# Foldings in pairs: two small weight products issued back to back instead of one at a time

## The chip, the cores and the metric

The kernel runs on one core of one Trainium2 chip. The metric is the time of one execution in device microseconds (us). The core's engines have queues of their own, each worked off in order: TensorE (PE in the profile, its weight loads PEld), VectorE (DVE), ScalarE (ACT), GpSimd (POOL) and SyncE (SP). Matrix products are written to PSUM, the memory behind TensorE, which is divided into banks; the other engines read them there.

## The reference, cut to what matters

Three stages follow each other on 8 batches of 576 tokens (8 heads of 64 in 512 columns):

```python
k_m = einsum('bhsm,bhsd->bhmd', a, k)          # a: softmax of phi over the tokens, 32 memories a head
v_m = einsum('bhsm,bhsd->bhmd', a, v)
attn = softmax(q @ k_m.T / 8)                  # 576 x 32 a head
x = attn @ v_m                                 # stage 1 input: 4608 x 512
x = (silu(x @ w_gate) * (x @ w_val)) @ w_out   # first feed-forward, 1536 hidden columns
out = elu(x @ w_in) @ w_out2                   # second feed-forward, 2048 hidden columns
```

The kernel never forms `attn @ v_m`. It multiplies `v_m` of a batch (the tile `vt`) into the gate and value weights (`WG`) first, and the result (`VW`) is then multiplied with `attn`. This small product is called a folding here.

## The kernel before, in words

A folding is `vw(b, p)`: for batch `b` and the pair `p` of hidden units (a unit is 128 hidden columns; units 0 to 3, pairs 0 and 1, belong to the first stage, pairs 2 to 5 to the second), eight matmuls of 64 rows by 32 columns write 128 x 1024 numbers into two PSUM banks (`pvw`). The profile counts each of the eight as two, so a folding is a row x16. Their shape uses a part of TensorE's array each, so that the eight work side by side; all matmuls of the feed-forwards use the whole array (128*128 in the rows). Then ScalarE copies the banks, rounded, into the upper half of `VW` (L265), and VectorE subtracts this copy from the banks for the lower half (L266). Only after the subtraction may TensorE write these banks again. There are 48 foldings, of which 46 are emptied in this way.

**First stage** (one pass for each batch `b`): gate and value products of units 0 to 3 (`pg`, `pv`, twice 6 matmuls of 288 columns for each unit and half), their output products (`pd`), and between them, one task after each unit's step (`todo`, `tick`), the attention of the next batches: transposes (`ps_aT`, `ps_kvT`), memories (`ps_kvm`), scores (`ps_sc`) and, at the end of the list, the two foldings for batch `b + 1` (`vw_tasks`). Both foldings use the bank pair `ps_kv` in turn. Scores use the bank pair `ps_at`.

**Second stage**: four runs `n` of two batches, 16 units each (`units`). The output product of run `n` is done in 14 steps (`down_steps`, a product of seven is two steps, `acc` in the rows, 24 matmuls a step: 12 for each of two token halves `hf`) and lies between the units of run `n + 1`. One unit is 12 `pg` matmuls, a Silu on ScalarE (L701), 12 `pv` matmuls and a product on VectorE (L703). In this mixture `pg`, `pv` and `pvw` take turns on two bank pairs (the list `turn`: 1, 0, 1, 0, ...), and `acc` holds the other two. After every second unit one folding is issued (`vw2`), for the pair of units that comes two pairs later. The rounded halves of what the output product reads are made ahead by ScalarE (`hh`, L767) and VectorE (`hl`, L768), and VectorE also forms the sums between operands (L771) and prepares the third stage's weights in the background (`uq`, `uw`, `wc`).

The framework's scheduler settles the order in each engine's queue before the kernel runs: it takes the instruction that is ready first in its own estimate of times, by rank among those that are ready. `tc.issue_after(x)` keeps what follows behind `x` in that order, and `tc.high_priority()` raises its rank. On the chip each queue is then worked off in exactly that order.

Of the kernel before, what the change touches and what calls it, by code (L numbers as in the profile page):

```python
# [8 lines left out]
F32 = mybir.dt.float32  # L9
F32R = mybir.dt.float32r  # L10
# [3 lines left out]
ALU = mybir.AluOpType  # L14
# [24 lines left out]
def attention_moe_moe(ctx: ExitStack, tc: tile.TileContext, qT, phiT, kv, kv4, w1g, w1o, w2, out):  # L39
# [208 lines left out]
    VW = {}  # L248
# [1 line left out]

    def vw(b, p, pool=None, ps=None):
        t = VW[b, p] = vx_p.tile([128, 2, 2, 512], F32R, tag="vx", name="vw")
        both = ps or pool.tile([128, 2, 512], F32, tag="at", name="pvw")
        ps = [both[:, g] for g in range(2)]

        def head(j, g):
            r, c = slice(64 * g, 64 * g + 64), slice(32 * j, 32 * j + 32)
            return mm(ps[g][c], lhsT=Bs[b].vt[r, j, :], rhs=WG[p][j][r], start=True, stop=True)  # L260

        together([lambda j=j, g=g: head(j, g) for j in reversed(range(KD)) for g in (1, 0)])
        if b >= NEG or p >= UA // 2:
            with tc.high_priority() if pool is None else nullcontext():
                act(out=t[:, 0], in_=both, func=AF.Copy)  # L265
                tt(out=t[:, 1], in0=both, in1=t[:, 0].bitcast(F32), op=ALU.subtract)  # L266
            return
        for g in range(2):
            last["vwh"] = act(out=t[:, 0, g, :], in_=ps[g], func=AF.Copy)
        for g in range(2):  # L270
            mm(ps[g], lhsT=minus, rhs=t[:, 0, g, :], start=False, stop=True, skip_group_check=True)
            last["vwl"] = act(out=t[:, 1, g, :], in_=ps[g], func=AF.Copy)
            if g == 0:
                last["vwl0"] = last["vwl"]
# [10 lines left out]
    def down(ps, w, hs, ms, start, stop, skip=False):  # L285
        mm(ps, lhsT=w[0][:, ms], rhs=hs[0], start=start, stop=False, skip_group_check=skip)  # L286
        mm(ps, lhsT=w[1][:, ms], rhs=hs[0], start=False, stop=False, skip_group_check=skip)  # L287
        mm(ps, lhsT=w[0][:, ms], rhs=hs[1], start=False, stop=stop, skip_group_check=skip)  # L288

    def split_h(pool, h, n):  # L290
        hh = pool.tile([128, n], F32R, tag="hh", name="hh")
# [228 lines left out]

    G2 = ps_kv

    def vw_tasks(b):
        for p in range(UA // 2):
            yield lambda p=p: vw(b, p, G2)
# [67 lines left out]
    for b in range(B):  # L593
# [32 lines left out]
        if b == 0:  # L626
            v = list(vw_tasks(1))
            todo += [bk[0], bk[1], v[0], lambda: Bs[2].phi(), bk[2], bk[3], bk[4], v[1], fr[0], fr[1], bk[5]] + fr[2:] + [lambda: Bs[3].phi()]
        else:
            for i in range(max(len(bk), len(fr))):  # L630
                todo += fr[i:i + 1] + bk[i:i + 1]
            if b + 1 < B:
                todo += vw_tasks(b + 1)
        done = [0, 0]
        spread = 18 if b == 0 else 16 if b < B - 2 else 24

# [61 lines left out]
    def unit2(b, u, out):  # L698
        pg = up2(b, u, 0, "pg")
        s = t_p.tile([128, 2, HS], F32, tag="s", name="s")  # L700
        last["gate"] = act(out=s, in_=pg, func=AF.Silu)  # L701
        pv = up2(b, u, 128, "pv")
        last["h"] = stt(out=out, in0=s, scalar=1.0, in1=pv, op0=ALU.mult, op1=ALU.mult)  # L703

    def vw2(b, p):
        if len(turn) > MIX:
            ps = bank2(3, "pvw")
        else:
            ps = bank2(turn.pop(0), "pvw")
        vw(b, p, ps=ps)  # L710


    held = {}
# [33 lines left out]
    def down_steps(n, g, steps, comb):  # L747
        acc = {}

        def step(j, name, r, k, chain, *dst):  # L750
            start = name in ("P1", "P2", "P5", "P4")[:4 if steps is ALONE else 3]
            if start and j == 0:
                acc[chain] = [bank2(i, "acc")[:, :, :HS] for i in ((0, 1) if chain == "D" else (2, 3))]
            behind = nullcontext() if steps is ALONE else tc.issue_after(unit_end[-LAG].ins)
            if steps is not ALONE:
                w = wo_p.tile([128, 2, 2, 256], F32R, tag="w", name="ws")
                nc.sync.dma_start(out=w.bitcast(F32), in_=d1_d[:, r, 2 * j:2 * j + 2])
            else:
                if j == 0:
                    acc["w"] = vx_p.tile([128, 4, 2, 256], F32R, tag="vx", name="ws")  # L760
                    last["ws"] = nc.sync.dma_start(out=acc["w"].bitcast(F32), in_=d1_d[:, r])
                w = acc["w"][:, 2 * j:2 * j + 2]
            for hf in range(2):
                hs = [hs_p.tile([128, 2, HS], F32R, tag=t, name=t) for t in ("hh", "hl")]
                x = g[k][:, hf, 2 * j:2 * j + 2]
                with tc.high_priority():
                    act(out=hs[0], in_=x, func=AF.Copy)  # L767
                    last["h"] = last["gate"] = tt(out=hs[1], in0=x, in1=hs[0].bitcast(F32), op=ALU.subtract)  # L768
                for o, a, b, f in comb.get((name, 2 * j + hf), []):
                    with tc.issue_after(last["h"].ins):  # L770
                        tt(out=g[o][:, f], in0=g[a][:, f], in1=g[b][:, f], op=ALU.add if (o, a, b) == (2, 2, 3) else ALU.subtract)  # L771
                for i, m in [(i, m) for i in range(2) for m in range(2)]:
                    with behind if hf + i + m == 0 else nullcontext():
                        down(acc[chain][m][:, hf], (w[:, i, 0], w[:, i, 1]), (hs[0][:, i], hs[1][:, i]),
                             slice(128 * m, 128 * m + 128), start and j + i == 0, j + i == 2, not start)
            if j == 1:
                add_part(acc[chain], [(2 * n + b, c) for b, c in dst],
                         name == "P4" if steps is ALONE else None)

        return [lambda a=a, j=j: step(j, *a) for a in steps for j in range(2)]  # L780
# [28 lines left out]
    load2(1)  # L809

    unit_end = []
    LAG = 1

    def units(n, g):
# [3 lines left out]
        def unit(i, k, u):  # L818
            b, p = pairs[8 * n + i]
            if u % UA == 0:  # L820
                g[k] = gh_p.tile([128, 2, UA, HS], F32, tag="gh", name="gh")
            unit2(b, u, g[k][:, :, u % UA])
            unit_end.append(last["pe"])
            done[0] += 1
            background(fs, n0 * (1 - done[0] / (12 if n == 0 else 16)))
            if u % 2 == 1:
                if 8 * n + i + 2 < len(pairs):
                    vw2(*pairs[8 * n + i + 2])
                if i in (5, 7) and n < B // 2 - 1:
                    load2(2 * n + 2 + i // 7, nc.gpsimd)  # L830

# [7 lines left out]
    for n in range(B // 2 - 1):  # L839
        us = units(n + 1, g[n + 1])  # L840
        for i, f in enumerate(down_steps(n, g[n], MIXED, MIXCOMB)):
            f()
            for _ in range(2 if i in (0, 12) else 1):
                us.pop(0)()
# [311 lines left out]
```

## Time and profile before

| what | value |
|---|---|
| median of 3 runs | 1426.08 us (1426.02 to 1429.0) |
| the profiled execution | 1427.93 us, span in the profile 1426.2 us |
| TensorE busy | 1401.3 us, 98% of the span |
| VectorE busy | 1136.1 us, 80% |
| ScalarE busy | 862.4 us, 60% |
| mean granted clock of TensorE | 0.995 of full speed |

The span runs from the first to the last instruction; the time of an execution has 1.7 us more around it. A busy share near 100% says that an engine has work issued nearly all the time. Where a stretch is meant, the view by stretches is the one to read: for each stretch it gives the time in it that each engine was busy.

### The profile page before, as it was taken

The page shows a single profiled execution, that of the slowest core. Times are in us where ns is not written, and L with a number is a line of the kernel's source. Part 1 is how long each engine was busy: PE and PEld are TensorE (multiplying, and loading weights), DVE is VectorE, ACT ScalarE, POOL GpSimd, SP SyncE. Part 2 cuts the span into 40 slices and gives each one's busy share as a digit, 9 for nine tenths or more (in the row PEclk, how much of TensorE's full clock was granted, in tenths as well). Part 3 has the DMA queues.
Part 4 walks back from the last instruction along what each step waited for, and adds up shares of the span by engine and source line. Part 5 has one row for each costly group of instructions (what it writes and reads, how often), then busy time and mean ns, then how long its engine had stood idle before and what let it go on. Part 6 is the DMA issues. An engine that isn't in the chain of part 4 may idle for free.

```text
span 1426.2 us, 23205 instructions
## 1 busy us (share of the span) xinstructions
PE 1401.3 (98%) x9259; PEld 1211.6 (85%) x9259; DVE 1136.1 (80%) x1452; ACT 862.4 (60%) x1254; POOL 44.8 (3%) x73
## 2 busy tenths in 40 slices
PE   6899999999999999999999999999999999999998
PEld 4787889988999999999988888888888888888887
DVE  7988978778798877877988578885889488957884
ACT  5665545544465555555666388557866587548843
POOL 0000000000000000000000000000000000000000
PEclk8999999999999999999999999999999999999999
DMA  9888512664789887888889756766686667566653
GB/s 378 326 298 292 208 72 101 230 233 175 237 251 309 284 240 232 274 241 287 267 291 364 269 188 206 280 214 189 201 282 219 190 202 265 215 210 203 213 201 132
DMA packets 89484, 337.65 MB, mean 237 GB/s; under 512 B 9376, under 2 KB 23712, under 8 KB 70048
## 3 DMA queue, kind: packets, MB, share of 16 engines
q1 hardware_dynamic: 55312, 254.04, 51.6%
q10 hardware_dynamic: 26880, 51.39, 9.8%
q0 software_dynamic: 7184, 30.74, 8.9%
q8 instruction: 73, 1.20, 0.3%
q14 instruction: 35, 0.29, 0.1%
HBM read 251.13 MB, written 85.00 MB: 236 GB/s over the span
## 4 chain that ended last, share of the span: by engine, by line
PE 93%; DVE 3%; ACT 2%; DMA 1%; issue 1%; ACTq 0%; SPq 0%; DVEq 0%
PE pu L877 12%; PE pu L879 12%; PE pu L878 12%; PE pd L877 5%; PE pd L879 5%; PE pd L878 5%; PE acc L288 4%; PE acc L286 4%; PE acc L287 4%; PE pv L281 3%; PE pg L281 3%; PE pv L283 3%; PE pv L282 3%; PE pg L283 3%; PE pg L282 3%; PE pvw L260 3%
## 5 line engine op out<-in xcount | busy, mean ns | idle before, releaser
L878 PE MATMUL pu<-xlo,w 128*128 128x512 f32 x672 | 261.4, 389 | 0.0
L877 PE MATMUL pu<-xhi,w 128*128 128x512 f32 x672 | 261.4, 389 | 0.0
L879 PE MATMUL pu<-xhi,w 128*128 128x512 f32 x672 | 261.4, 389 | 0.0
L906 ACT ACTIVATE xhi<-g 128x1024 fp32r<-128x1024 f32 x120 | 126.5, 1058 | 106.9 <-PE pu L879 64.3
L907 DVE TENSOR_TENSOR xlo<-g,xhi 128x1024 fp32r<-128x1024 f32 x120 | 145.0, 1220 | 40.7 <-ACT xhi L906 40.6
L879 PEld LDWEIGHTS pu<-xhi,w 128*128 128x128 f32 x672 | 126.1, 188 | 26.3
L878 PEld LDWEIGHTS pu<-xlo,w 128*128 128x128 f32 x672 | 126.1, 188 | 26.2
L877 PEld LDWEIGHTS pu<-xhi,w 128*128 128x128 f32 x672 | 126.1, 188 | 26.1
L287 PE MATMUL acc<-hh,ws 128*128 128x288 f32 x448 | 131.7, 296 | 0.0
L286 PE MATMUL acc<-hh,ws 128*128 128x288 f32 x448 | 131.5, 295 | 0.0
L288 PE MATMUL acc<-hl,ws 128*128 128x288 f32 x448 | 128.8, 297 | 0.0
L281 PE MATMUL pv<-at,vw 128*128 128x288 f32 x384 | 115.6, 301 | 2.4 <-DVE s L306 0.7
L281 PE MATMUL pg<-at,vw 128*128 128x288 f32 x384 | 116.7, 304 | 1.1 <-ACT p L579 0.5
L767 ACT ACTIVATE hh<-gh 128x576 fp32r<-128x576 f32 x112 | 76.0, 685 | 68.6 <-PE acc L287 50.8
L282 PE MATMUL pg<-at,vw 128*128 128x288 f32 x384 | 114.1, 297 | 0.9 <-DVE at L488 0.9
L283 PE MATMUL pg<-at,vw 128*128 128x288 f32 x384 | 113.6, 296 | 0.0
L282 PE MATMUL pv<-at,vw 128*128 128x288 f32 x384 | 113.6, 296 | 0.0
L283 PE MATMUL pv<-at,vw 128*128 128x288 f32 x384 | 113.5, 296 | 0.0
L877 PE MATMUL pd<-xhi,w 128*128 128x512 f32 x288 | 112.0, 389 | 0.0
L878 PE MATMUL pd<-xlo,w 128*128 128x512 f32 x288 | 112.0, 389 | 0.0
L879 PE MATMUL pd<-xhi,w 128*128 128x512 f32 x288 | 112.0, 389 | 0.0
L897 DVE SCALAR_TENSOR_TENSOR et<-et 128x1024 f32<-128x1024 f32 x72 | 87.8, 1219 | 28.8 <-ACT et L896 28.8
(161 smaller groups left out, 3226.9 us busy)
## 6 DMA issues: line engine op xcount, KB each, us to landing
w<-dnd SPq DMA_DIRECT2D x64, 1024.0 KB, 4.9
w<-upd SPq DMA_DIRECT2D x40, 1024.0 KB, 5.7
w<-upd SPq DMA_DIRECT2D x32, 768.0 KB, 4.6
ws<-d1d SPq DMA_DIRECT2D x42, 512.0 KB, 4.5
kvr<-kv SPq DMA_DIRECT2D x32, 512.0 KB, 7.5
wr<-w SPq DMA_DIRECT2D x16, 1024.0 KB, 6.3
upd<-uw ACTq DMA_DIRECT2D x32, 512.0 KB, 6.3
dnd<-uw ACTq DMA_DIRECT2D x32, 512.0 KB, 7.9
```

The lines of the kernel that those rows point to most:

```text
L281: mm(ps, lhsT=wh, rhs=ah, start=g == 0, stop=False)
L282: mm(ps, lhsT=wh, rhs=al, start=False, stop=False)
L283: last["pe"] = mm(ps, lhsT=wl, rhs=ah, start=False, stop=g == 1)
L286: mm(ps, lhsT=w[0][:, ms], rhs=hs[0], start=start, stop=False, skip_group_check=skip)
L287: mm(ps, lhsT=w[1][:, ms], rhs=hs[0], start=False, stop=False, skip_group_check=skip)
L288: mm(ps, lhsT=w[0][:, ms], rhs=hs[1], start=False, stop=stop, skip_group_check=skip)
L877: mm(ps, lhsT=w[0], rhs=x[0], start=start, stop=False, skip_group_check=skip)
L878: mm(ps, lhsT=w[0], rhs=x[1], start=False, stop=False, skip_group_check=skip)
L879: last["mm"] = mm(ps, lhsT=w[1], rhs=x[0], start=False, stop=stop, skip_group_check=skip)
L897: stt(out=a, in0=e, scalar=1.0, in1=a, op0=ALU.add, op1=ALU.mult)
L906: last["hi"] = act(out=hi, in_=x, func=AF.Copy)
L907: last["lo"] = tt(out=lo, in0=x, in1=hi.bitcast(F32), op=ALU.subtract)
```

## The change

In the first stage, from batch 2 on, both foldings of a batch are issued in one go, 16 matmuls in a row, into two different bank pairs (`ps_kv` and `ps_at`), and emptied one after the other. In the second stage, single foldings after every second unit remain only in run 0. In the steps 2, 4, 8 and 11 of each output product two pairs of units are folded at once: after the first 12 matmuls of the step, into both bank pairs of the turn, the first folding in the bank that the next `pg` will take, the second in that of the next `pv`. The last steps have no pairs left to fold.

```diff
+    def vw_both(b):
+        ps = [pool.tile([128, 2, 512], F32, tag="at", name="pvw") for pool in (G2, ps_at)]
+        together([c for p, t in enumerate(ps) for c in vw_calls(b, p, t)])
+        for p, t in enumerate(ps):
+            vw_out(b, p, t, G2)
...
             if b + 1 < B:
-                todo += vw_tasks(b + 1)
+                todo += [lambda: vw_both(b + 1), lambda: None]
...
-    def vw2(b, p):
-        if len(turn) > MIX:
-            ps = bank2(3, "pvw")
-        else:
-            ps = bank2(turn.pop(0), "pvw")
-        vw(b, p, ps=ps)
+    def vw2(*of):
+        at = [3] if len(turn) > MIX else [turn.pop(0) for _ in range(3)][1::-1]
+        ps = [bank2(i, "pvw") for i in at]
+        together([c for bp, t in zip(of, ps) for c in vw_calls(*bp, t)])
+        for bp, t in zip(of, ps):
+            vw_out(*bp, t)
...
                 for i, m in [(i, m) for i in range(2) for m in range(2)]:
+                    if hf == 1 and i + m == 0 and folds:
+                        with tc.issue_after(last["acc"].ins), tc.issue_after(last["pv"].ins):
+                            vw2(*folds)
+                        folds.clear()
...
+    folds = []
+    FOLD = {2: 2, 4: 4, 8: 6, 11: 8}
...
             if u % 2 == 1:
-                if 8 * n + i + 2 < len(pairs):
-                    vw2(*pairs[8 * n + i + 2])
+                if n == 0:
+                    vw2(pairs[i + 2])
...
         for i, f in enumerate(down_steps(n, g[n], MIXED, MIXCOMB)):
+            if i in FOLD:
+                folds.extend(pairs[8 * n + 8 + FOLD[i]:8 * n + 10 + FOLD[i]])
             f()
```

`vw_calls` holds the eight matmuls of the old `vw`, `vw_out` its copy and subtraction, unchanged.

The order in which the built programs stand shows where the foldings went. **First stage, TensorE, the foldings of batch 3** (`pvw`; `ps_kvT` is the transpose of another batch's memories ahead of them, `pd` and `pv` are feed-forward products, `ps_aT` another transpose). Before, the first of the two stands behind the transposes and the second behind a value product, some fifty rows later:

```order
L410 MATMUL ps_kvT_1615<-ident_143,kvm_1549 128x128 x2
L260 MATMUL pvw_1704<-wg_294,vt_1141 32x512 x4
L260 MATMUL pvw_1704<-wg_279,vt_1141 32x512 x4
L286 MATMUL pd_1599<-hh_1286,woh_419 128x288
L287 MATMUL pd_1599<-hh_1286,wol_420 128x288
```

```order
L282 MATMUL pv_1715<-at_1024,vw_1239 128x288
L283 MATMUL pv_1715<-at_1024,vw_1239 128x288
L260 MATMUL pvw_1729<-wg_332,vt_1141 32x512 x4
L260 MATMUL pvw_1729<-wg_325,vt_1141 32x512 x4
L380 MATMUL ps_aT_1935<-ident_143,ph_1472 128x128 x2
```

Now both stand together:

```order
L416 MATMUL ps_kvT_1615<-ident_143,kvm_1549 128x128 x2
L257 MATMUL pvw_1703<-wg_294,vt_1141 32x512 x4
L257 MATMUL pvw_1703<-wg_279,vt_1141 32x512 x4
L257 MATMUL pvw_1704<-wg_332,vt_1141 32x512 x4
L257 MATMUL pvw_1704<-wg_325,vt_1141 32x512 x4
L292 MATMUL pd_1599<-hh_1286,woh_419 128x288
```

The second folding moved up to the first. It is so for batches 2, 3 and 4; for batches 5, 6 and 7 other matmuls still stand between the two.

**Second stage, TensorE, the third pair of run 0's output product.** Before, the first of these two foldings stands between output products and a value product:

```order
L286 MATMUL acc_5118<-hh_5630,ws_5612 128x288
L287 MATMUL acc_5118<-hh_5630,ws_5612 128x288
L288 MATMUL acc_5118<-hl_5631,ws_5612 128x288
L260 MATMUL pvw_5687<-wg_4059,vt_1141 32x512 x4
L260 MATMUL pvw_5687<-wg_3797,vt_1141 32x512 x4
L281 MATMUL pv_5661<-at2_4770,vw_5358 128x288
```

Now the two follow each other, and the gate product `pg_5671`, which writes the bank of `pvw_5635`, comes five matmuls later:

```order
L292 MATMUL acc_5108<-hh_5730,ws_5712 128x288
L257 MATMUL pvw_5635<-wg_4059,vt_1141 32x512 x4
L257 MATMUL pvw_5635<-wg_3797,vt_1141 32x512 x4
L257 MATMUL pvw_5636<-wg_4279,vt_1141 32x512 x4
L257 MATMUL pvw_5636<-wg_4098,vt_1141 32x512 x4
L293 MATMUL acc_5108<-hh_5730,ws_5712 128x288
L294 MATMUL acc_5108<-hl_5731,ws_5712 128x288
L292 MATMUL acc_5108<-hh_5730,ws_5712 128x288
L293 MATMUL acc_5108<-hh_5730,ws_5712 128x288
L294 MATMUL acc_5108<-hl_5731,ws_5712 128x288
L287 MATMUL pg_5671<-at2_4770,vw_5324 128x288
```

Between a pair and the next `pg` there stand 12 matmuls at the pairs in steps 2 and 4 of every run, 5, 9 and 9 at the pairs of step 8 in runs 0, 1 and 2, and 24 at the two pairs of step 11 (runs 0 and 1). The `pv` that takes the second folding's bank stands directly behind that `pg`, but for step 8 of run 0, where 12 `acc` matmuls lie between.

**Second stage, VectorE, the pair in step 2 of run 1** (`vw` are the subtractions; `uq` and `uw` background work, `hl` operands of the output product, `gh` the product of a unit). Before, the first of these two is one subtraction amid other work:

```order
L703 SCALAR_TENSOR_TENSOR gh_6183<-s_6236,pv_6238 128x2x288
L168 TENSOR_TENSOR uq_6213<-uq_6213,wc_6214 128x1024
L266 TENSOR_TENSOR vw_6259<-pvw_6258,vw_6259 128x1024
L233 TENSOR_TENSOR uw_6252<-uq_6213,uw_6252 128x2x256
L233 TENSOR_TENSOR uw_6255<-uq_6213,uw_6255 128x2x256
```

Now both subtractions are near each other, with two background instructions between them:

```order
L780 TENSOR_TENSOR hl_6528<-gh_4953,hh_6527 128x576
L228 TENSOR_TENSOR uq_6214<-uq_6214 128x256
L229 TENSOR_TENSOR uq_6214<-uq_6214 128x256
L272 TENSOR_TENSOR vw_6380<-pvw_6362,vw_6380 128x1024
L233 TENSOR_TENSOR uw_6332<-uq_6214,uw_6332 128x2x256
L233 TENSOR_TENSOR uw_6335<-uq_6214,uw_6335 128x2x256
L272 TENSOR_TENSOR vw_6383<-pvw_6363,vw_6383 128x1024
L715 SCALAR_TENSOR_TENSOR gh_6184<-s_6411,pv_6413 128x2x288
```

The second subtraction moved up to the first, and what lies between them is part of the way to its bank's release. In run 2 the same two `uw` stand there. In step 2 of run 0 it is L229 and one `uw`; in step 4 of run 0 it is L168, in step 4 of runs 1 and 2 L131; in steps 8 and 11 nothing.

## Rows read from the trace of the kernel before

**Rows 1.** The page, busy time of the engines.

```profile
PE 1401.3 (98%) x9259; PEld 1211.6 (85%) x9259; DVE 1136.1 (80%) x1452; ACT 862.4 (60%) x1254; POOL 44.8 (3%) x73
```

**Rows 2.** By stretches: us, busy PE, PEld, DVE, ACT, POOL; granted clock; DMA.

```profile
30.00:298.00 268.00, 261.94 (x2637) 227.67 (x2637) 230.40 (x430) 155.62 (x338) 0.00 (x0) 1.00 0.62 225
...
366.00:680.80 314.80, 314.56 (x2524) 291.03 (x2523) 256.86 (x330) 174.04 (x263) 20.04 (x25) 1.00 0.86 261
```

**Rows 3.** Instructions on `pvw`: count, shortest/median/longest ns, first and last start.

```profile
L260 PEld LDWEIGHTS pvw<-wg,vt x768: 102/106/151, 20.5 to 661.1; 64*32 64x32 f32 x192
L260 PE MATMUL pvw<-wg,vt x768: 589/589/1059, 20.5 to 661.5; 64*32 64x512 f32 x192
```

**Rows 4.** Timeline, TensorE around one second-stage folding: start, duration, instruction.

```profile
474.30 0.29 PE L287 MATMUL acc<-hh,ws 128*128 128x288 f32 x1
474.44 0.29 PE L288 MATMUL acc<-hl,ws 128*128 128x288 f32 x1
474.66 1.09 PE L260 MATMUL pvw<-wg,vt 64*32 64x512 f32 x16
475.68 0.40 PE L286 MATMUL acc<-hh,ws 128*128 128x288 f32 x1
475.92 0.30 PE L287 MATMUL acc<-hh,ws 128*128 128x288 f32 x1
```

**Rows 5.** Timeline, TensorE: a folding directly behind scores.

```profile
95.78 0.29 PE L288 MATMUL pd<-hl,woh 128*128 128x288 f32 x1
...
96.44 0.72 PE L445 MATMUL ps_sc<-qr,kT 64*32 64x288 f32 x16
96.95 1.06 PE L260 MATMUL pvw<-wg,vt 64*32 64x512 f32 x16
...
98.19 0.29 PE L282 MATMUL pg<-at,vw 128*128 128x288 f32 x1
```

**Rows 6.** Timeline, TensorE: scores without a folding behind them.

```profile
101.11 0.29 PE L288 MATMUL pd<-hl,woh 128*128 128x288 f32 x1
...
101.77 0.71 PE L445 MATMUL ps_sc<-qr,kT 64*32 64x288 f32 x16
...
102.66 0.30 PE L282 MATMUL pg<-at,vw 128*128 128x288 f32 x1
```

**Rows 7.** Timeline, all engines: the shortest way from a folding to its bank's release.

```profile
462.69 1.09 PE L260 MATMUL pvw<-wg,vt 64*32 64x512 f32 x16
...
463.89 1.03 ACT L265 ACTIVATE vw<-pvw 128x1024 fp32r<-128x1024 f32 x1 [3.09 <-PE pvw L260]
...
464.94 1.22 DVE L266 TENSOR_TENSOR vw<-pvw,vw 128x1024 fp32r<-128x1024 f32 x1
...
465.81 0.29 PE L283 MATMUL pg<-at,vw 128*128 128x288 f32 x1
...
466.22 0.19 PEld L281 LDWEIGHTS pv<-at,vw 128*128 128x128 f32 x1 [0.35 <-DVE vw L266]
```

**Rows 8.** The same view, the longest such way.

```profile
422.35 1.09 PE L260 MATMUL pvw<-wg,vt 64*32 64x512 f32 x16
...
426.00 1.22 DVE L266 TENSOR_TENSOR vw<-pvw,vw 128x1024 fp32r<-128x1024 f32 x1
```

**Rows 9.** The same view, the middle one of 23.

```profile
555.25 1.09 PE L260 MATMUL pvw<-wg,vt 64*32 64x512 f32 x16
...
558.03 1.23 DVE L266 TENSOR_TENSOR vw<-pvw,vw 128x1024 fp32r<-128x1024 f32 x1 [0.70 <-ACT vw L265]
```

**Rows 10.** Timeline, VectorE: spacing of queued instructions.

```profile
433.65 0.42 DVE L229 TENSOR_TENSOR uq<-uq 128x256 f32<-128x256 f32 x1
433.98 0.68 DVE L233 TENSOR_TENSOR uw<-uq,uw 128x512 fp32r<-128x512 f32 x1
...
487.69 1.23 DVE L266 TENSOR_TENSOR vw<-pvw,vw 128x1024 fp32r<-128x1024 f32 x1 [0.46 <-ACT vw L265]
488.84 1.28 DVE L233 TENSOR_TENSOR uw<-uq,uw 128x512 fp32r<-128x512 f32 x2
```

More of the change, by code (lines that the diff above doesn't have):

```diff
@@ L249, in attention_moe_moe, with vw_calls, vw, vw_out @@
     raw = {}
[L253 to L256, printed above, removed]
+    def vw_calls(b, p, ps):
         def head(j, g):
             r, c = slice(64 * g, 64 * g + 64), slice(32 * j, 32 * j + 32)
-            return mm(ps[g][c], lhsT=Bs[b].vt[r, j, :], rhs=WG[p][j][r], start=True, stop=True)
-        together([lambda j=j, g=g: head(j, g) for j in reversed(range(KD)) for g in (1, 0)])
+            return mm(ps[:, g][c], lhsT=Bs[b].vt[r, j, :], rhs=WG[p][j][r], start=True, stop=True)
+        return [lambda j=j, g=g: head(j, g) for j in reversed(range(KD)) for g in (1, 0)]
+    def vw(b, p, pool=None, ps=None):
+        both = ps or pool.tile([128, 2, 512], F32, tag="at", name="pvw")
+        together(vw_calls(b, p, both))
+        vw_out(b, p, both, pool)
+    def vw_out(b, p, both, pool=None):
+        t = VW[b, p] = vx_p.tile([128, 2, 2, 512], F32R, tag="vx", name="vw")
+        ps = [both[:, g] for g in range(2)]
         if b >= NEG or p >= UA // 2:
@@ L287, in down @@
         mm(ps, lhsT=w[1][:, ms], rhs=hs[0], start=False, stop=False, skip_group_check=skip)
-        mm(ps, lhsT=w[0][:, ms], rhs=hs[1], start=False, stop=stop, skip_group_check=skip)
+        last["acc"] = mm(ps, lhsT=w[0][:, ms], rhs=hs[1], start=False, stop=stop, skip_group_check=skip)
     def split_h(pool, h, n):
@@ L702, in unit2 @@
         pv = up2(b, u, 128, "pv")
-        last["h"] = stt(out=out, in0=s, scalar=1.0, in1=pv, op0=ALU.mult, op1=ALU.mult)
-    def vw2(b, p):
-        if len(turn) > MIX:
-            ps = bank2(3, "pvw")
-        else:
-            ps = bank2(turn.pop(0), "pvw")
-        vw(b, p, ps=ps)
+        last["pv"] = last["h"] = stt(out=out, in0=s, scalar=1.0, in1=pv, op0=ALU.mult, op1=ALU.mult)
+    def vw2(*of):
[4 more added lines that the diff above has]
+            vw_out(*bp, t)
     held = {}
```

## The prediction

> **What bounds the kernel now.** The page's busy times come first: TensorE is busy for 98% of the span, VectorE for 80% [rows 1]. By stretches, TensorE is busy for 261.9 of 268.0 us of the first stage and for 314.6 of 314.8 us of the mixture in the second, at the full clock, with VectorE at 230.4 and 256.9 us [rows 2]. So TensorE sets the end in both places that the change touches: whatever it issues costs its time, and whatever it waits for is added. VectorE is its closest neighbour, busy for 82% of the mixture.
>
> **What a folding costs TensorE.** From one output matmul at 474.44 over a folding to the second matmul behind it at 475.92 it is 1.48 us [rows 4]. The matmuls of 288 columns follow each other at 0.13 to 0.14 us [rows 4], 0.133 over a longer stretch, a dozen in 1.60; two take 0.27, so the folding takes 1.21. It starts 0.22 after the matmul ahead of it instead of 0.133, the next matmul starts 1.02 after it, and the one behind that another 0.24. A part of the 1.21 is change of shape. How large a part is seen where a folding stands directly behind the scores, which have the same 64*32 shape. From the last `pd` to the second `pg` it takes 98.19 - 95.78 = 2.41 us with scores and folding [rows 5], and 102.66 - 101.11 = 1.55 with scores alone [rows 6]; four transposes stand ahead of the scores in both. There the folding costs 0.86, and 0.35 is saved.
>
> **What the change removes.** Two foldings in a row should cost 1.21 + 0.86 on TensorE. Eleven pairs stand together in the second stage, three in the first (batches 2 to 4). The order also puts a set of scores directly ahead of a memory product once in the first stage, which saves about as much again, but takes away the folding behind scores of rows 5. So 14 x 0.35 = 4.9 us are saved. Batches 5 to 7 save nothing.
>
> A rule of the Trainium skill speaks against this term: in TensorE: Matmul & The Clock Gate, Part 3, The mechanism, weight loads overlap running matmuls only if they go to other rows of the array. The second folding's loads go to the rows that the first one uses. A load takes 0.106 us [rows 3]; if by that rule the first load of each of two row groups in each of two passes stood free, 0.42 us of estimate would take the whole saving of a pair. Rows 5 do not bear this out: scores and folding share rows too, and the folding behind them cost only 0.86.
>
> **What it moves.** No arithmetic is added: ScalarE copies and VectorE subtracts as often as before. No DMA is moved on a queue that anything here waits for. But a bank pair comes free only when its subtraction ends, and that is where TensorE waits. One such wait is in the trace already: the folding at 462.69 is copied from 463.89 (1.20 later), subtracted from 464.94 (2.25 later) to 466.16, and `pv`, due one pitch after 465.81, at 465.94, starts at 466.22, with VectorE's subtraction named as releaser [rows 7]. Release is thus 1.28 after the subtraction's start. The wait is small because in this order the folding's bank is needed only by the next tile but one: in between there is a whole `pg` in the other bank.
>
> With a pair there is no other bank. The next `pg` takes the first folding's bank, the next `pv` the second's. Counted from the pair's start, TensorE is at the first matmul behind it after 0.86 + 1.02 = 1.88 us. With N `acc` matmuls until `pg` it is there after 1.88 + 0.24 + (N - 1) x 0.133: 3.58 for N = 12, 3.19 for 9, 2.65 for 5, 5.18 for 24.
>
> The first bank is released L + 1.28 after the start, with L the time from a folding's start to its subtraction. Over the 23 foldings of the mixture L is between 2.25 [rows 7] and 3.65 [rows 8], the middle one 2.78 [rows 9]; above the least value it is ScalarE or VectorE that is late. I take the middle, since nothing but the number of foldings changes in these queues. Release is then at 4.06, and `pg` waits 0.48 (N = 12), 0.87 (9), 1.41 (5), and not at all with 24.
>
> The second bank: VectorE's next 1024-wide instruction follows after 1.15, a `uw` takes 0.60 in a queue, L229 0.33 [rows 10]. So the second release comes 1.15 plus whatever stands between the subtractions after the first. `pv` follows `pg` after 1.60, so it waits for what stands between, less 0.45:
>
> - step 2: run 0 (L229 and one `uw`, 0.93) 0.48; runs 1 and 2 (two `uw`, 1.20) 0.75 each
> - step 4: run 0 (L168, 1.15) 0.70; runs 1 and 2 (L131, about as long as a `uw`) 0.15 each
> - steps 8 and 11: 0.
>
> Sums: step 2 has 3 x 0.48 + 1.98 = 3.4; step 4 has 3 x 0.48 + 1.00 = 2.4; step 8 has 1.41 + 2 x 0.87 = 3.2. Together 9.0 us.
>
> Bounds by the two ends of L: with 2.25 `pg` waits only at step 8 (0.88, 0.34, 0.34) and `pv` some 0.05 less each time, 4.3 us in all. With 3.65 (release at 4.93) `pg` waits 1.35, 1.74 and 2.28, 16.8 us in all. Two waits like that of rows 7 vanish with the foldings that caused them (0.28 each), 0.6.
>
> In the first stage I cost the waits at nothing: behind each of the three pairs the next scores, which take the second bank, come after at least 24 feed-forward matmuls, 3.2 us behind the pair's 1.88, against a second release at 2.78 + 1.28 + 1.15 = 5.21. If that cover were gone, each would cost up to a microsecond. What is queued behind a waiting `pg` or `pv` is all of TensorE's work; Silu, products and operand halves follow later by as much, and nothing gives it back, since TensorE has no idle time in the mixture.
>
> **Sum.** -4.9 - 0.6 + 9.0 = +3.5 us. The profiled execution took 1427.9, 1.8 above the median of 1426.1, so its 1431.4 stand for a median of 1429.6 us, 0.25% slower.
>
> **Rivals.**
>
> 1. *The banks are free in time, and the change gains.* While TensorE waits, ScalarE and VectorE catch up, and background work between subtractions could find them ahead. For it: VectorE has 58 us without work in the mixture [rows 2]. Against it: even with VectorE never late the sum above leaves 4.3. The gain is over 0.2% (2.85 us) only if waits stay below 2.6 us, thus only if the first subtraction starts well before 2.25, or `pg` comes later than its place says. Without any wait: 1426.1 - 5.5 = 1420.6.
> 2. *L is at its least throughout.* -5.5 + 4.3: 1424.9, no measurable change.
> 3. *VectorE is later than the middle.* Two subtractions of 1.22 [rows 7] now come together, at steps 2 and 4 close to the sums between operands (L771), and `hl` behind them may come late too. -5.5 + 16.8: 1437.4.
> 4. *The second folding's loads stand free,* so that nothing is saved: 9.0 - 0.6, thus 1434.5. Its rule is the skill's, named above; rows 5 speak against it.
>
> **How the numbers follow.** A measurement of this kernel tells some 0.2% (2.85 us) from no change. My forecast, waits of 7 to 12 us, has a chance of 0.42; its own range is 1427.5 to 1433, about two thirds of it slower by over 0.2%. Rival 1 has 0.25, rival 2 0.15, rival 3 0.13, rival 4 0.05. Slower: 0.27 + 0.13 + 0.05 = 0.45; same: 0.15 + 0.15 = 0.30; faster: 0.25. The range 1421.5 to 1435.5 leaves out the better third of rival 1 and most of rival 3.
>
> **What would show it.** TensorE's time over a pair (from the matmul ahead to the second behind) should be 2.07 + 0.27 us; if it is 2.7, the saving is not there. At steps 2, 4 and 8 weight loads of `pg` and `pv` should show idle time released by the subtraction (L272 there), of 0.2 to 1.4 us, some 15 in all; at step 11 none. The mixture should be some 4 us longer, the first stage 1 us shorter. I am wrong if the pairs' subtractions start at 2.3 us or less and TensorE shows no such waits, or if `acc` waits for `hl` instead.

## The result, and the profile after

The changed kernel takes 1447.77 us (median of 4 runs, 1446.63 to 1449.62) where the kernel before takes 1427.05 in the same session: a ratio of 1.0146, with a 95% interval of 1.0131 to 1.0161. That is 20.7 us slower. The forecast was 3.5 us slower, with a range up to 1435.5: the sign was right, the time is outside the range.

The profiled execution took 1446.63 us with a span of 1444.9 us, 18.7 more than before. Three starts on TensorE split this. The last `pd` (end of the first stage) starts at 316.52 us instead of 308.67, 7.9 later. From the first `acc` to the last one (mixture and the product done alone) it takes 382.7 us instead of 371.2, 11.5 more. Between these two it takes 0.7 us less, and from the last `acc` to the end 699.2 us, before 699.1. So both places that the change touches lost time, and nothing else did. The prediction had -1 for the first and +4.5 for the second.

The page's busy times, as in [rows 1]:

```profile
PE 1404.7 (97%) x9259; PEld 1215.2 (84%) x9259; DVE 1137.4 (79%) x1452; ACT 861.5 (60%) x1254; POOL 44.8 (3%) x73
```

and the two stretches of [rows 2] in the changed kernel:

```profile
30.00:298.00 268.00, 256.85 (x2577) 223.08 (x2583) 222.71 (x416) 147.62 (x326) 0.00 (x0) 0.99 0.59 213
366.00:680.80 314.80, 303.93 (x2437) 281.21 (x2437) 249.81 (x320) 167.80 (x251) 19.18 (x24) 1.00 0.81 251
```

All engines have nearly as much work as before over the whole span, but TensorE is now without any for 11.2 us of the first stretch and 10.9 of the second, before 6.1 and 0.2. No engine got more to do: TensorE waits. (The stretches are fixed in time, so the changed kernel is a little less far in them.)

**The saving is there.** The timeline of TensorE around the pair in step 2 of run 1 (start, duration, instruction):

```profile
506.24 0.29 PE L294 MATMUL acc<-hl,ws 128*128 128x288 f32 x1
506.47 1.95 PE L257 MATMUL pvw<-wg,vt 64*32 64x512 f32 x32
...
508.58 0.30 PE L293 MATMUL acc<-hh,ws 128*128 128x288 f32 x1
```

From 506.24 to 508.58 it is 2.34 us, the 2.07 + 0.27 of the forecast. Ten of the eleven pairs cost this; the other one waits ahead of its first matmul. In TensorE: Matmul & The Clock Gate, Part 3, The mechanism, the Trainium skill lists that loads overlap running matmuls only if they go to other rows; the second folding's loads go to the rows of the first, and this trace does not agree. The same section also lets loads into a background weight buffer go ahead of running matmuls; that would fit, but no row here shows which buffer a load goes to.

**Second stage.** What TensorE waits for between 362 and 721 us (view of waits: engine, line, releaser; total us, times, longest):

```profile
PE pg L287 <- DVE vw L272: 5.2, 7, 1.4
PE acc L294 <- DVE hl L780: 1.9, 3, 0.7
PE pv L287 <- DVE vw L272: 1.6, 4, 0.5
PE acc L292 <- ACT ev L741: 0.7, 1, 0.7
PE pg L287 <- ACT s L713: 0.7, 1, 0.7
PE pvw L257 <- DVE gh L715: 0.5, 1, 0.5
```

The 11 waits of `pg` and `pv` for the subtraction are the ones forecast. The other six had no price in its sum. In rows like these a wait also costs about 0.26 us more than its idle time: in the rows of the first stage below, `pd` at 259.47 starts 0.83 after the matmul ahead of it where 0.13 is the pitch, 0.70 lost for 0.53 shown, and the matmul behind a wait comes 0.23 to 0.24 later instead of 0.13 (260.17 to 260.40). The first part is a matter of reading: a row is 0.29 long, the next one starts 0.13 after it, and idle time counts from the row's end. So 10.6 us shown and 17 x 0.26 are 15.0 us; less 11 x 0.35 saved and less the two waits of before (0.6), 10.5 of the 11.5 us are accounted for.

The pair in step 8 of run 1 in the timeline of all engines, from which rows are left out:

```profile
550.07 1.95 PE L257 MATMUL pvw<-wg,vt 64*32 64x512 f32 x32
...
551.14 1.21 DVE L132 SCALAR_TENSOR_TENSOR wc<-wr,wc 128x1024 f32<-128x1024 uint32 x1
...
551.26 1.94 ACT L271 ACTIVATE vw<-pvw 128x1024 fp32r<-128x1024 f32 x2 [0.93 <-PE pvw L257]
...
552.38 1.23 DVE L168 TENSOR_TENSOR uq<-uq,wc 128x1024 f32<-128x1024 f32 x1
...
553.53 2.35 DVE L272 TENSOR_TENSOR vw<-pvw,vw 128x1024 fp32r<-128x1024 f32 x2
...
554.80 0.40 PE L287 MATMUL pg<-at,vw 128*128 128x288 f32 x1 [1.40 <-DVE vw L272]
```

ScalarE copies 1.19 after the pair's start, as early as in [rows 7]. VectorE could subtract some 2.3 after it, but two 1024-wide background instructions (`wc`, `uq`) stand ahead in its queue: L is 3.46, not the 2.78 of the forecast.

Step 4 of the same run is worse, since there an operand is late too:

```profile
522.11 1.95 PE L257 MATMUL pvw<-wg,vt 64*32 64x512 f32 x32
...
523.97 1.21 DVE L129 SCALAR_TENSOR_TENSOR uq<-uq,wc 128x1024 int32<-128x1024 int32 x1
...
525.11 0.75 DVE L780 TENSOR_TENSOR hl<-gh,hh 128x576 fp32r<-128x576 f32 x1
...
525.77 1.21 DVE L272 TENSOR_TENSOR vw<-pvw,vw 128x1024 fp32r<-128x1024 f32 x1
...
525.91 0.40 PE L294 MATMUL acc<-hl,ws 128*128 128x288 f32 x1 [0.59 <-DVE hl L780]
...
527.04 0.40 PE L287 MATMUL pg<-at,vw 128*128 128x288 f32 x1 [0.35 <-DVE vw L272]
```

A background step (L129) and `hl` stand ahead of the subtraction, which starts 3.66 after the pair; `acc` waits for `hl` and then `pg` for the bank.

**First stage.** What TensorE waits for from 64 us to the end of the stage, in the changed kernel:

```profile
PE pd L292 <- DVE h L319: 2.4, 2, 2.1
PE pg L287 <- DVE s L312: 1.6, 3, 0.7
...
```

With seven waits for `p`, `hl`, `kvm` and `s` these are 7.8 us in 12 waits, before 2.7 in 6. None is for a folding's bank. All but that for `kvm` are waits of the feed-forward products for VectorE and ScalarE, and eight of the 12 come from 199 us on. The largest, with TensorE's matmuls around it:

```profile
258.64 0.29 PE L293 MATMUL pd<-hh,wol 128*128 128x288 f32 x1
259.47 0.40 PE L294 MATMUL pd<-hl,woh 128*128 128x288 f32 x1 [0.53 <-DVE hl L300]
260.17 0.40 PE L287 MATMUL pv<-at,vw 128*128 128x288 f32 x1 [0.30 <-DVE s L312]
260.40 0.29 PE L288 MATMUL pv<-at,vw 128*128 128x288 f32 x1
...
263.32 0.61 PE L292 MATMUL pd<-hh,woh 128*128 128x288 f32 x1 [2.11 <-DVE h L319]
263.73 0.44 PE L293 MATMUL pd<-hh,wol 128*128 128x288 f32 x1
```

The wait of 2.11 us for `h` does not begin at VectorE. In the same stretch, ScalarE and VectorE:

```profile
260.54 1.12 ACT L127 ACTIVATE wg<-wr 128x1024 f32<-128x1024 f32 x1 [2.01 <-DMA wr<-w1g]
...
261.56 0.62 ACT L232 ACTIVATE uw<-uq 128x512 fp32r<-128x512 f32 x1
...
262.21 0.69 DVE L233 TENSOR_TENSOR uw<-uq,uw 128x512 fp32r<-128x512 f32 x1 [2.10 <-ACT uw L232]
```

ScalarE's queue stands 2.01 us at a background step whose weights are still being loaded (`wg`), the copy `uw` comes behind it, VectorE stands 2.10 us for that copy, and `h` is next in its queue, at 262.82. The kernel before has the same stop of ScalarE, 1.40 us until 258.91, but the only wait of TensorE near it is one of 0.47 us (260.39).

The granted clock around this wait (stretch, its length, busy times, clock in the third column from the end):

```profile
260.00:265.00 5.00, 2.72 (x13) 2.50 (x14) 2.87 (x7) 3.22 (x6) 0.00 (x0) 0.79 1.02 405
265.00:270.00 5.00, 5.00 (x35) 5.00 (x35) 1.82 (x4) 1.77 (x6) 0.00 (x0) 0.87 0.75 286
```

After the waits of 0.53, 0.30 and 2.11 us the granted clock is 0.79 and 0.87 of full speed in the two stretches, that is, at the lower of its two levels (1.2 and 2.4 GHz) for a part of them, and a matmul of 288 columns shows 0.44 us instead of 0.29. Ten of them from 263.73 on follow each other at 0.24 us instead of 0.13; with the ones at both ends this takes another 1.3 us, until 266.35. Waits (5.1 more, and 6 more of them at 0.26), clock (1.3) and three pairs (-1.05 by the forecast's price) give 6.9 of the 7.9 us; the end of the stage itself is known to 1 or 2 us (see the table below).

### The profile page after: what moved, and what is told of

Same layout as the page of the kernel before. It is cut to its first block, busy times and chain, and to the rows that moved or that the text cites. A ratio compares the mean times of both kernels' runs of the same rounds, so it can differ in the third digit from the quotient of the medians.

```text
span 1444.9 us, 23203 instructions
## 1 busy us (share of the span) xinstructions
PE 1404.7 (97%) x9259; PEld 1215.2 (84%) x9259; DVE 1137.4 (79%) x1452; ACT 861.5 (60%) x1254; POOL 44.8 (3%) x73
## 4 chain that ended last, share of the span: by engine, by line
PE 84%; DVE 8%; DMA 4%; issue 2%; ACT 2%; SPq 0%; ACTq 0%; DVEq 0%
PE pu L898 12%; PE pu L897 12%; PE pu L899 12%; PE pd L898 5%; PE pd L897 5%; PE pd L899 5%; PE acc L292 4%; PE acc L293 4%; PE acc L294 3%; PE pg L287 3%; PE pv L287 3%; PE pv L289 3%; PE pv L288 3%; PE pg L288 3%; PE pg L289 3%; DMA wr<-w1g 2%
```

## The experiments

The comparisons by stage, in us. "End of stage 1" is the start of the last `pd`; "mixture" is from the first to the last `acc`; the scores are the starts of the first half of batches 6 and 7.

| kernel | median | ratio, 95% interval | end of stage 1 | mixture | scores 6, 7 |
|---|---|---|---|---|---|
| before | 1427.05 | | 308.7 | 371.2 | 169.2, 192.9 |
| changed | 1447.77 | 1.0146 [1.0131, 1.0161] | 316.5 | 382.7 | 187.1, 218.5 |
| e1_first | 1435.97 | 1.0061 [1.0043, 1.0079] | 317.3 | 371.3 | 187.8, 219.2 |
| e2_second | 1440.18 | 1.0085 [1.0069, 1.0100] | 310.1 | 383.9 | |
| e3_first234 | 1428.37 | 1.0004 [0.9994, 1.0013] | 308.7 | 371.2 | 159.3, 193.3 |
| e4_cover | 1441.35 | 1.0095 [1.0070, 1.0120] | 307.5 | 387.6 | |
| e6_banks | 1438.66 | 1.0066 [1.0045, 1.0087] | 320.3 | 371.3 | 191.0, 222.4 |
| e7_order | 1426.95 | 0.9990 [0.9981, 1.0000] | 307.7 | 371.3 | 168.3, 192.0 |
| e8_quiet | 1433.43 | 1.0035 [1.0022, 1.0047] | 307.7 | 375.1 | 168.5, 192.2 |
| e9_late | 1436.83 | 1.0068 [1.0051, 1.0085] | 317.0 | 371.2 | 191.7, 222.0 |
| e10_best | 1447.84 | 1.0139 [1.0122, 1.0156] | 307.2 | 392.4 | |
| e11_scores | 1433.62 | 1.0045 [1.0030, 1.0060] | 315.0 | 371.2 | 188.0, 220.8 |
| e12_two | 1437.25 | 1.0071 [1.0055, 1.0088] | 307.5 | 381.5 | 168.2, 191.9 |

Each ratio is taken against runs of the kernel before in the same session (medians 1427.05 to 1428.66). A stage that an experiment leaves as before has its old length in every row (mixture 371.2 to 371.3; the first stage ends at 307.2 to 310.1, which is how well its end is known).

### Which stage loses: e1_first and e2_second

Each keeps one half of the change; the other half is as before. (Wherever the second stage is as before, and in e4_cover, e8_quiet, e10_best and e12_two, a single folding again takes one bank pair.)

In e1_first:

```diff
-    FOLD = {2: 2, 4: 4, 8: 6, 11: 8}
+    FOLD = {}
...
-                if n == 0:
-                    vw2(pairs[i + 2])
+                if 8 * n + i + 2 < len(pairs):
+                    vw2(pairs[8 * n + i + 2])
```

In e2_second:

```diff
-                todo += [lambda: vw_both(b + 1), lambda: None]
+                todo += vw_tasks(b + 1)
```

> The first stage's foldings in pairs, the second stage as before the change. Theory A (the loss adds up by stages, and the first stage's part comes from the order around the foldings of batches 5 to 7): the first stage ends some 8 us later than before, as in the changed kernel (316.5 against 308.7 us), the mixture is as long as before, the whole is 7 to 8 us slower than before, about 1434. Rival B (the prediction's sum; the first stage loses only together with the rest): 1 us faster than before, 1425 to 1426.

> The second stage's foldings in pairs, the first stage as before the change. Theory A: the first stage ends as before at 308.7 us, the mixture and the last product together are 12 to 13 us longer than before, the whole is 11 to 13 us slower, 1438 to 1440. Rival B (the prediction's terms for the second stage are right, 9.0 of waits less 4.5): 1431 to 1432.

Measured: 8.3 and 12.5 us slower than before in that session, together the 20.7 of the change. The two losses add up; the prediction's sum was wrong in both stages.

### Pairs only where they stand together: e3_first234

```diff
-                todo += [lambda: vw_both(b + 1), lambda: None]
+                todo += [lambda: vw_both(b + 1), lambda: None] if b < 4 else list(vw_tasks(b + 1))
```

> First stage only, and pairs only for batches 2, 3 and 4, where the two foldings really stand together; batches 5 to 7 and the second stage as before. Theory A (the moved foldings of batches 5 to 7 are what costs): three pairs save 0.35 each and nothing waits, 1425 to 1426. Rival C (the pairs of batches 2 to 4 themselves bring the loss, through the bank pair of the scores): the first stage ends 3 to 8 us late as in the changed kernel, 1430 to 1435.

Measured: no difference, and the stage ends at 308.7 as before. The three pairs are not what costs. The expected 1 us gain did not show either: three waits of 0.4 to 0.8 us for `s`, `h` and `hl` came in at 166 to 171 us.

### Banks or order: e6_banks and e7_order

The first stage's change is two edits: the second folding goes to the scores' bank pair, and both are issued in one task. Each is made alone.

In e6_banks, with the task list of before:

```diff
-            yield lambda p=p: vw(b, p, G2)
+            yield lambda p=p: vw(b, p, (G2, ps_at)[p] if b > 1 else G2)
```

In e7_order:

```diff
-                todo += [lambda: vw_both(b + 1), lambda: None]
+                todo += [lambda: (vw(b + 1, 0, G2), vw(b + 1, 1, G2)), lambda: None]
```

> First stage only: the two foldings of a batch are two tasks as before the change, but the second one goes to the bank pair of the scores, as in the changed kernel. Second stage as before. Theory F (the loss of batches 5 to 7 comes from the second folding sharing the scores' banks, so that scores and transposes move): the first stage ends 4 to 8 us later than before, 1431 to 1435. Rival G (it comes from issuing both in one task at the place of the first): the first stage ends within 1.5 us of before, 1426 to 1429.

> First stage only: both foldings of a batch are issued in one task, as in the changed kernel, but both use the old bank pair in turn, so that the second can only follow the first one's subtraction. Second stage as before. Theory G (the place in the list of tasks costs): the first stage ends 4 to 8 us later than before, 1431 to 1435. Rival F (the scores' banks cost): within 1.5 us of before, 1426 to 1429. If neither of the two kernels is late, it takes both edits together.

Measured: the banks alone cost as much as the first stage's whole change, without a single pair; the order alone costs nothing (0.9990, at the edge of what is told from no change). So it is the scores' banks. Why shows in the changed kernel's timeline of batch 5's foldings and the next scores:

```profile
154.78 1.09 PE L257 MATMUL pvw<-wg,vt 64*32 64x512 f32 x16
...
158.24 1.09 PE L257 MATMUL pvw<-wg,vt 64*32 64x512 f32 x16
...
172.09 1.03 ACT L271 ACTIVATE vw<-pvw 128x1024 fp32r<-128x1024 f32 x1 [0.32 <-PE pv L289]
...
181.60 1.01 ACT L271 ACTIVATE vw<-pvw 128x1024 fp32r<-128x1024 f32 x1
...
183.22 1.19 DVE L272 TENSOR_TENSOR vw<-pvw,vw 128x1024 fp32r<-128x1024 f32 x1
...
187.11 0.72 PE L451 MATMUL ps_sc<-qr,kT 64*32 64x288 f32 x16
```

The first copy, 17 us behind its folding, is released by a `pv` matmul, not by the folding: there are four `VW` tiles, two for each batch, and the copy needs one that older products still read. The second subtraction starts 25 us behind its folding. In the kernel before, that folding is issued 19 us later (177.69) and its subtraction starts at the same 183.22: the tile sets this time, not the folding. In the old bank pair that costs nothing, since the next folding there is far off; in the scores' banks the scores of batch 6 stand behind it and come at 187.1. In the kernel before, batch 5's first folding (at 166.37) is copied at 171.72, released by a `pv` too, but the scores of batch 6 pass it:

```profile
169.17 0.72 PE L445 MATMUL ps_sc<-qr,kT 64*32 64x288 f32 x16
...
171.72 1.03 ACT L265 ACTIVATE vw<-pvw 128x1024 fp32r<-128x1024 f32 x1 [0.39 <-PE pv L283]
```

### A short stay in the scores' banks: e9_late

```diff
-        together([c for p, t in enumerate(ps) for c in vw_calls(b, p, t)])
+        with tc.issue_after(begin.ins):
+            together([c for p, t in enumerate(ps) for c in vw_calls(b, p, t)])
...
+        begin = last.get("pe")
```

`begin` is set at the start of each pass, to the last product of the pass ahead of it.

> First stage only, all six pairs in the old bank pair and the scores' bank pair as in the changed kernel, but a batch's pair is issued only behind the last feed-forward product of the pass that uses up the tiles its results go to. Second stage as before. Theory I (a folding issued early holds the scores' banks until one of the four VW tiles is free; with the pairs in the first stage alone the second folding of batch 5 started at 159.0 and its subtraction at 183.9, 25 us later): the way from a pair to its second subtraction stays under 8 us, the scores come no later than some 5 us after their place of before, and the first stage ends between 2 us earlier and 1 us later than before: 1426 to 1429. Rival J (any folding in the scores' banks costs, however short it stays): the first stage ends 4 to 8 us late, 1432 to 1436.

Measured: 1436.8, 0.8 above rival J's range; the first stage ends 8.3 us late. The stay is short now (under 6 us from each pair to its second subtraction), but the scores are as late as ever:

```profile
180.72 1.95 PE L257 MATMUL pvw<-wg,vt 64*32 64x512 f32 x32
...
185.05 1.21 DVE L272 TENSOR_TENSOR vw<-pvw,vw 128x1024 fp32r<-128x1024 f32 x1
...
191.68 0.71 PE L451 MATMUL ps_sc<-qr,kT 64*32 64x288 f32 x16
```

So theory I fell: what counts is not the length of the stay, but that the scores stand behind a folding at all, and with it behind the pass that frees its tile. Whether the folding waits for the tile in the bank or ahead of it makes no difference that shows here (317.0 and 316.5).

### Late scores without any pair: e11_scores

```diff
-        yield lambda: z.score(0)
+        def score0():
+            with tc.issue_after(marks[b - 2].ins) if b > 5 else nullcontext():
+                z.score(0)
+        yield score0
```

`marks` holds the last `pv` of the second unit of each pass.

> No folding is paired and no bank changed: the kernel before, but the scores of batches 6 and 7 are held back behind the fourth gate or value product of the pass before the one that issues them, which puts them some 18 to 27 us later than before (they started at 169.2 and 192.9 us in the kernel before, at 187.8 and 219.2 with pairs in the first stage alone). Theory L (the first stage's loss is the attention of the late batches, which can no longer run ahead of the feed-forward products once its scores share banks with a folding, and which then crowds VectorE and ScalarE in the last passes): the first stage ends 5 to 9 us late, 1432 to 1437, without a single pair. Rival M (the lateness of the scores is harmless; the foldings in the scores' banks cost by themselves): within 1.5 us of before, 1426 to 1429.

Measured: 1.0045, the first stage ends 6.3 us late. Nothing but the place of the scores of two batches is changed, and the waits are like those of the changed kernel (64 to 315 us):

```profile
PE pd L292 <- DVE h L319: 3.0, 2, 2.8
...
```

The longest, 2.8 us, is at the same `pd` (263.15), behind the same stop of ScalarE. The late place of the scores is the cause, and it makes up most of the loss. How it leads to each of the waits was followed only for this one. What is left (the stage ends at 316.5 to 320.3 with foldings in the scores' banks, at 315.0 here) was not taken apart; in the changed kernel 1.3 us of it is the clock, which stayed at 1.00 here.

### More matmuls behind the pair: e4_cover

The unit behind the pairs of steps 2, 4 and 8 is held back into the next step, and the single folding at the end of run 0 takes one bank.

```diff
+                late = nullcontext()
+                if hf == 1 and mid:
+                    with tc.issue_after(last["acc"].ins):
+                        mid.pop(0)()
+                    late = tc.issue_after(unit_end[-1].ins)
...
+            if i in (2, 4, 8):
+                mid.append(us.pop(0))
+                continue
```

> Second stage only, with the pairs, but the unit that follows the pairs of steps 2, 4 and 8 is held back into the next step, so that 18 output matmuls and not 12 stand between most of these pairs and the next gate product (0.8 us more); the single folding at the end of run 0 takes one bank as before. First stage as before. Theory A (TensorE waits for the two banks): the waits of gate products behind pairs at steps 2 and 4 shrink from about 0.5 to nothing, those of step 8 from 1.2 to 1.6 by about 0.8 in runs 1 and 2, and the mixture is 5 to 8 us shorter than with the pairs as they are: 1431 to 1435. Rival D (VectorE and ScalarE have become too late for everything, so that waits only move on to operand halves and value products): no shorter than the kernel with pairs in the second stage alone, 1438 to 1440.

Measured: no gain. The waits for `vw` did shrink (3.7 us, from 6.8 in e2_second; at step 8 by the 0.8 expected, 1.07 to 0.32 and 1.40 to 0.6), but output products moved forward by a unit, and there `ev` and the load of `ws` were late:

```profile
PE acc L292 <- ACT ev L744: 4.3, 1, 4.3
PE acc L292 <- DMA ws<-d1d: 3.2, 3, 2.5
PE pg L287 <- DVE vw L272: 2.2, 5, 0.6
PE pv L287 <- DVE vw L272: 1.5, 3, 0.5
...
```

The time is near rival D's, but not by its mechanism alone: the experiment brought in waits of its own and does not separate the theories. Its four runs also lie far apart, 1438.0 to 1444.4, and the trace is of one at 1443.9.

### VectorE free around the pairs: e8_quiet

```diff
-        for after in last.get("h"), first.get("ex"):
+        for after in last.get("h"), first.get("ex"), last.get("sub2"):
...
-            background(fs, n0 * (1 - done[0] / (12 if n == 0 else 16)))
+            if not quiet:
+                background(fs, n0 * (1 - done[0] / (12 if n == 0 else 16)))
...
+            quiet[:] = [i] if i in (0, 1, 2, 3, 6, 7, 9, 10) else []
```

`sub2` is the last subtraction of a folding, and a single folding takes one bank. The list of quiet steps also holds 6, 7, 9 and 10, so background work is moved ahead of steps 8 and 11 too, which the expectation does not say.

> Second stage only, with the pairs; the background work on the third stage's weights is not issued around steps 2 and 4 and goes behind the subtractions, so that in those steps VectorE has no background instruction before or between the two subtractions; at step 8 it has as before. The single folding at the end of run 0 takes one bank as before the change. First stage as before. Theory E (TensorE's waits are VectorE's lateness): from a pair's start to its first subtraction it takes 2.3 to 2.8 us at steps 2 and 4 and some 3.5 at step 8; the waits of steps 2 and 4, some 7.6 us in the kernel with pairs in the second stage alone, fall below 2.5, those of step 8 stay at 1.2 to 1.6; the waits of 2.2 us behind the single folding vanish; 1432 to 1434. Rival H (the window between two units is too short for a pair even with VectorE free): waits of steps 2 and 4 stay at 5 us or more, 1437 to 1438.

Measured: 1.0035, 4.8 us slower than before in its session, where e2_second was 12.5 slower; the mixture is 8.7 us shorter than in e2_second. The pair in step 2 of run 1:

```profile
493.79 1.95 PE L257 MATMUL pvw<-wg,vt 64*32 64x512 f32 x32
...
496.07 2.35 DVE L272 TENSOR_TENSOR vw<-pvw,vw 128x1024 fp32r<-128x1024 f32 x2 [0.16 <-ACT vw L271]
```

L is 2.28 here, and 2.25 to 2.46 at all pairs of steps 2 and 4; `pg` and `pv` wait for nothing. All that TensorE waits for in its mixture:

```profile
PE pg L289 <- DVE vw L272: 1.9, 3, 0.6
PE pg L289 <- ACT s L715: 1.7, 1, 1.7
PE pv L289 <- DVE gh L717: 0.9, 1, 0.9
```

The first line is step 8, where 8 matmuls stand behind the pair. The other two are new; that background work, pushed together elsewhere, made `s` and `gh` late there is likely, but was not followed up. Theory E holds at steps 2 and 4. At step 8, where I expected an L of 3.5 still, it was 2.57, and the waits fell from 1.1 to 1.4 to 0.6. The edit reached this step as well: one background instruction (`wc`, L132) now stands directly ahead of the first subtraction instead of two.

### Putting the rest together: e10_best and e12_two

Both take e7_order's first stage and pairs with quiet steps: e10_best in steps 2, 4 and 11, e12_two in steps 2 and 4, with single foldings in the other places. The diff is e10_best's; in e12_two `FOLD` lacks step 11 and the singles have 4 to 7.

```diff
+    FOLD = {2: 2, 4: 4, 11: 8}
...
+                if 8 * n + i + 2 < len(pairs) and (n == 0 or i in (4, 5)):
+                    vw2(pairs[8 * n + i + 2])
...
+            quiet[:] = [i] if i in (0, 1, 2, 3) else []
```

> What the experiments leave of the change, put together: in the first stage both foldings in one task in the old bank pair (as in the kernel that was 1.7 us faster than before in its runs), in the second stage pairs only in steps 2, 4 and 11, single foldings in the place of the pairs of step 8, no background work on VectorE around steps 2 and 4, and one bank for the single folding at the end of run 0. Theory (a pair gains 0.35 us where its banks come free in time): eight pairs save 2.8, waits at them stay below 0.2 each, 1422 to 1426 with the first stage's part. Rival K (the background work, pushed together elsewhere, makes other operands late, as two waits of 1.1 and 1.9 us did in the kernel with quiet steps): 1427 to 1430.

> First stage: both foldings of a batch in one task in the old bank pair. Second stage: pairs in steps 2 and 4 only, with no background work on VectorE around them, single foldings for the rest, one bank for the single folding at the end of run 0. Theory (a pair gains where VectorE subtracts at once): six pairs save 2.1, no waits at them, 1423 to 1426. Rival K (the background work, pushed together in the later steps, makes other operands late there): 1427 to 1434.

Measured: both are worse than before, beyond rival K's range. In both `acc` waits 6 us for `hh` near the end of the mixture, since ScalarE's queue stands at a background copy whose tile waits for a store:

```profile
703.66 0.63 ACT L232 ACTIVATE uw<-uq 128x512 fp32r<-128x512 f32 x1 [6.70 <-DMA dnd<-uw]
```

That row is of e10_best, in which the pair of step 11 also stood directly behind a single folding and waited 1.6 us for its bank, and `pv` then 2.7. Moving background work is not free in these two, and no version here beats the kernel before by more than e7_order's 0.1%, which is itself at the edge of no change.

## Why the prediction was wrong, step by step

- **TensorE's saving, 0.35 us a pair: right.** 2.34 us over a pair, as forecast; rival 4 is out.
- **"In the first stage I cost the waits at nothing": the step that failed most.** It took the second release, 5.21 us behind the pair, from the second stage [rows 7, 9]. That held for batches 2 and 3 (5.1 and 5.2), not for batch 4 (12.6, by which e3_first234 lost nothing). The batches that it left out ("Batches 5 to 7 save nothing") are where the release came far later, in batch 5 some 26 us behind the folding, because the copy waits for a `VW` tile. The trace of the kernel before had shown this already: batch 6's first folding, at 190.09, is subtracted at 206.88. And it asked whether TensorE would wait at the scores. TensorE never does: the scheduler puts the scores of batches 6 and 7 some 18 and 26 us later in its order, and the wait is paid elsewhere, by feed-forward products for `s`, `h` and `p` (e6_banks, e9_late and e11_scores show this). The term was 0 for waits, and measured is about +9, the lower clock included.
- **L = 2.78 in the second stage: wrong at steps 4 and 8.** It was 2.25 to 3.18 at step 2, 3.7 to 4.2 at step 4, and at step 8 2.59 in run 0 and 3.46 in runs 1 and 2, near or above the upper bound [rows 8]. I had written that nothing but the number of foldings changes in these queues; but a pair stands at a fixed place among the sums, `hl` and the background work, so that a middle over singles at other places does not hold for it. The rest of the working holds: with L = 3.46 it has `pg` start 1.55 us late at step 8, and it started 1.56 late (554.80). All 11 waits for the subtraction together delay a start by 8.6 us, near the forecast's 9.0, but by luck: 2.2 for 3.4 at step 2, 2.1 for 2.4 at step 4, where the wait for `hl` ahead of `pg` hides a part, and 4.3 for 3.2 at step 8. Rival 3 had the late VectorE right, but its 16.8 us for these waits is not what they cost.
- **`hl` late: named, but not priced.** Three waits at step 4, 1.9 us shown, 2.4 by the starts. With it `acc` waits for `hl` instead of `pg` for the bank, one of the signs that I had given of being wrong.
- **A wait's price.** I counted how late a waiting matmul starts, but not that the matmul behind it comes another 0.10 us later, 1.7 us over the 17 waits.
- **The single folding at the end of run 0: missed.** In the new `vw2` a single one also takes three turns, two bank pairs; behind it (377.73) `acc` waits 0.74 for `ev` and `pg` 0.74 for `s`. In e8_quiet, where it takes one, both waits are gone. Before the pair in step 4 of run 0 (413.35) stands the last of the six waits without a price, 0.52 for `gh`.
- **Step 11 free of waits, third stage untouched: right.**

## What to carry to other kernels

Before a product moves to another buffer, ask who else uses that buffer and what its own results wait for: two streams that ran at different distances ahead are tied together, and the price shows where neither of them stands. A release time measured in one stage is no release time for another, and a middle over many places is none for a fixed place: read what stands in the queue there. An engine that is busy for 82% of the time still decides when it empties a bank late, and moving its background work out of the way can move the lateness with it (e10_best and e12_two).

## What was not expected of the hardware

A wait of TensorE costs more than the trace shows as idle: 0.70 us for 0.53 shown, and 0.1 more on the next matmul. The first 0.17 comes from how the rows are drawn, which overlap by 0.16 when nothing waits; the 0.1 stood behind 16 of the 17 waits of the second stage.

The granted clock fell behind waits that were not long. In the changed kernel TensorE waited 0.53, 0.30 and 2.11 us within 5 us, and then matmuls followed each other at 0.24 us instead of 0.13 from 263.73 to 266.35 although none waited; the two stretches of 5 us show 0.79 and 0.87. In e9_late a single wait of 2.50 us (`pg` at 137.64), with no other close ahead of it, was followed by 0.85 and 0.81 in the two stretches from 135 to 145 us. In e11_scores a single wait of 2.76 us (`pd` at 263.15) left it at 1.00. So these rows do not tell by the length or the number of the waits when the clock falls. The Trainium skill, TensorE: Matmul & The Clock Gate, Part 1, What's actually happening, has an idle engine fall from the higher of the two clocks to the lower; the changed kernel and e9_late agree, and e11_scores shows that not every such wait brings it. It cost about 1.3 us in the changed kernel.
